# A gated long-convolution backward pass: a key product summed in half-partition VectorE operations, and a PSUM operand in place of an evacuation

## The chip, the cores and the metric

The kernel runs on one core of one Trainium2 chip. The metric is the device time of one execution in microseconds (us). Its engines, as the profile names them: PE is TensorE's matmuls, PEld its weight loads, DVE is VectorE, ACT is ScalarE, POOL is GpSimd, SP issues transfers. Single executions of the kernel before lie within 1.5 us of each other (555.2 to 556.7 us). Each trace is of one execution. The granted clock is the share of full speed that the chip allows TensorE; in before's runs its mean is 0.998 to 1.000.

## The reference, cut to what matters

A forward pass and the gradients of nine of its inputs, in bf16. The forward pass normalises `x`, runs a long convolution over the sequence (2048 positions, 512 channels) by FFT, and gates the result with a sigmoid MLP (512 to 1376 to 512):

```python
kv_f = rfft(k_shift * v, padded)                 # V spectrum
kf_f = rfft(ssm_k, padded)                       # K spectrum (filter)
y    = irfft(kv_f * kf_f)[:S] + kv * ssm_D       # complex product per frequency
s    = q * y                                     # q is the normalised x
g    = silu((sigmoid(xn @ w_gate) * (xn @ w_up)) @ w_down)
out  = x + s * g                                 # then the vector-Jacobian product for grad_out
```

The kernel does the FFTs as matmuls with cosine and sine blocks. Real and imaginary parts lie in the two halves of the 128 partitions, so a complex product is two elementwise products, whose parts have to be added up across the halves. Either the inverse step's matmuls do that (two matmuls per block, one per product), or VectorE does it with half-partition operations, and one matmul per block is enough.

## The kernel before: what the change and the argument touch

Instructions are not emitted as written. A recording layer collects all operations with their dependencies, and a list scheduler lays them out, engine by engine, at build time; the chip then runs that fixed order. Some evacuations may be dealt to ScalarE or VectorE (`evac`), and the parts of the kernel are streams that advance at set paces against each other.

```python
HALF = (1,)                       # which of KK's two halves is summed on VectorE in the backward stage
def evac(self, dst, src, n):      # the scheduler chooses the engine
    self.add([("scalar", "copy", (dst, src), {}), ("vector", "tensor_copy", (dst, src), {})])

def step3(Qf, qq, which, dst):    # second FFT step: 2 matmuls of 512 columns, one evacuation of 1024
    ps = ps_mm([2, 512]); ...     # ps_mm: one of three double PSUM banks in this stage
    nc.evac(dst, ps[:]..., 1024)

def inv3(terms, qq, Bg):          # first inverse step: 8 blocks, one matmul of 128 columns per term
    for g in range(8):
        for n, (Y, r) in enumerate(terms): nc.tensor.matmul(ps[:, g], Y[:, g*128:(g+1)*128], R[:, r], ...)
    nc.evac(...)

def strX():                       # FFT stage: four groups (cg) of four quarter steps (qq)
    for cg in range(NG):
        for qq in range(4): ... step3(QfK, qq, X_RI, KFg[:, qq])        # K spectrum
        for qq in range(5):
            step3(QfV, qq, X_RI, Xc); Y  = Xc * KFg[:, qq]
            step3(QfV, qq, X_IR, Xs); Xs = Xs * KFg[:, qq]              # second product, from SBUF
            inv3(((Y, R_A), (Xs, R_B)), qq - 1, Bg)                     # of the quarter before
        inv1(...)
run_streams([(gG, len(FA) * 11776, 0.05, 0.7), (strK(), 4 * 10240, 0.0, 0.7), (strV(), 4 * 16384, 0.0, 0.8),
             (strX(), 4 * 24576 + 4096, 0.2, 1.0)])     # gG: ten tiles of the gate's matmuls, the filler

def backC():                      # backward stage, beside a stream of weight-gradient matmuls (filler)
    for cg in range(NG):
        for qq in range(5): ...   # two step3 (Xr, Xi), then for KK's halves t = 0, 1:
            # t not in HALF: T2 = K*Xi; K = K*Xr, full height, inv3 with two terms
            # t in HALF: four half-partition products and a sum, inv3 with one term
```

## Time and profile before

556.4 us. The table is worked out from the trace: the price of the matmuls that start in a stretch at 56, 149 and 216 ns for 128, 352 and 512 columns, and the bubbles, the rest of the time from one matmul's start to the next. Time is counted from the first busy instruction, 0.2 us after the trace's span begins; the first matmul starts 2.0 us later, and these 2.0 us stand in no row.

| stretch, us | stage | matmuls at their price | bubbles |
|---|---|---|---|
| 0 to 21 | start-up | 8.4 | 10.7 |
| 21 to 142 | FFT stage, gate tiles beside it | 107.5 | 13.5 |
| 142 to 190 | its end, start of the gated stage | 43.5 | 4.7 |
| 190 to 345 | gated stage | 154.0 | 0.8 |
| 345 to 516 | backward stage | 170.0 | 1.0 |
| 516 to 554 | weight gradients alone | 32.9 | 5.2 |

How to read it: a bubble is the time by which the next matmul starts later than the price says, so the time before the first matmul, the prices and the bubbles make up the whole time. The page's chain that ended last says the same in shares of the span:

```profile
PE 77%; ACT 8%; issue 7%; DVE 5%; POOL 1%; DMA 1%; POOLq 0%; ACTq 0%
```

TensorE carries three quarters of it, and ScalarE's 8% lie almost all before 190 us.

### The profile page before, as it was taken

The numbers are of one execution on the slowest core, as the hardware profiler recorded it, in microseconds if no ns is written. First come the engines' busy times: TensorE is split into PE (matmuls) and PEld (weight loads), VectorE is DVE, ScalarE is ACT, GpSimd is POOL, SyncE is SP. The second block draws the span as 40 slices with busy tenths as digits, with TensorE's granted clock in tenths as the row PEclk, the third lists the DMA queues.
The fourth block names the chain that finished last, engine by engine and source line by source line (L and its number), as shares of the span: only waits on it lengthen the run. The fifth ranks groups of instructions, "written<-read, shape, count | busy, mean of one in ns | idle before, by whom it ended". The sixth has DMA issues, their size and how long they took to land.

```text
span 554.4 us, 13669 instructions
## 1 busy us (share of the span) xinstructions
PE 531.3 (96%) x5613; PEld 377.8 (68%) x5613; DVE 445.1 (80%) x867; ACT 354.1 (64%) x465; POOL 140.6 (25%) x250
## 2 busy tenths in 40 slices
PE   3999899999989999999999999999999999999996
PEld 2999697898778566777665675656756756666544
DVE  9588999856897999889898899739769879798620
ACT  7989999978996234455343445359767858765311
POOL 3234323303212322222232111311041052131221
PEclk9999999999999999999999999999999999999999
DMA  8879889729434898989979979998695588878431
GB/s 288 238 210 279 269 230 295 197 72 282 155 115 111 221 198 211 276 170 201 272 192 274 257 194 301 277 289 238 188 287 174 180 273 254 244 223 247 153 114 37
DMA packets 125288, 120.37 MB, mean 217 GB/s; under 512 B 74963, under 2 KB 104489, under 8 KB 125226
## 3 DMA queue, kind: packets, MB, share of 16 engines
q1 hardware_dynamic: 109946, 71.22, 50.9%
q0 software_dynamic: 14752, 48.27, 27.4%
q8 instruction: 44, 0.72, 0.6%
q14 instruction: 18, 0.15, 0.1%
q10 hardware_dynamic: 528, 0.00, 0.0%
HBM read 54.23 MB, written 47.55 MB: 184 GB/s over the span
## 4 chain that ended last, share of the span: by engine, by line
PE 77%; ACT 8%; issue 7%; DVE 5%; POOL 1%; DMA 1%; POOLq 0%; ACTq 0%
PE psum L515 77%; ACT slab L515 8%; DVE slab L515 5%; POOL out_dram L515 1%; DMA slab<-in_grad_out_dram 1%; POOL slab L515 0%; ACT L515 0%; POOLq L1447 0%; POOLq L515 0%; ACTq L515 0%; POOLq L1436 0%
## 5 line engine op out<-in xcount | busy, mean ns | idle before, releaser
L515 PE MATMUL psum<-slab 128*128 128x128 bf16 (+4 forms) x5613 | 531.3, 257 | 18.6 <-ACT slab L515 11.8
L515 PEld LDWEIGHTS <-slab 128*128 128x128 bf16 (+2 forms) x5613 | 377.8, 102 | 171.8 <-issue 17.6
L515 DVE TENSOR_TENSOR slab<-slab 128x512 bf16<-128x512 bf16 (+5 forms) x507 | 293.6, 623 | 13.9 <-ACT slab L515 6.4
L515 ACT CAST slab<-psum 128x1024 bf16<-128x1024 f32 (+4 forms) x262 | 217.6, 875 | 78.0 <-PE psum L515 68.7
L515 ACT COPY slab<-psum 128x1024 bf16<-128x1024 bf16 (+2 forms) x90 | 75.6, 862 | 90.6 <-PE psum L515 90.4
L515 POOL DMA_DIRECT2D out_dram<-slab x75 | 44.1, 591 | 190.5 <-DVE slab L515 101.9
L515 DVE TENSOR_TENSOR slab<-psum,slab 128x512 bf16<-128x512 f32 (+2 forms) x68 | 44.5, 655 | 26.1 <-PE psum L515 16.3
L515 ACT ACTIVATE slab<-slab 128x512 bf16<-128x512 bf16 (+3 forms) x46 | 36.6, 803 | 15.6 <-DVE slab L515 15.1
L515 ACT ACTIVATE slab<-psum 128x512 bf16<-128x512 f32 (+1 forms) x64 | 37.6, 593 | 11.1 <-PE psum L515 7.7
L515 DVE CAST slab<-psum 128x1024 bf16<-128x1024 f32 (+1 forms) x27 | 31.7, 1181 | 10.2 <-PE psum L515 10.0
L515 DVE SCALAR_TENSOR_TENSOR slab<-slab 128x1 f32<-128x1 f32 (+3 forms) x64 | 28.0, 437 | 12.9 <-ACT slab L515 12.1
L515 POOL DMA_DIRECT2D KK_d<-slab x32 | 17.4, 544 | 58.1 <-ACT slab L515 52.0
L515 POOL DMA_DIRECT2D slab<-in_A_q_dram x29 | 16.0, 553 | 47.2 <-DMA out_dram<-slab 33.2
L515 DVE COPY slab<-psum 128x1024 bf16<-128x1024 bf16 (+1 forms) x26 | 17.1, 667 | 12.8 <-PE psum L515 12.5
L515 DVE TENSOR_SCALAR slab<-slab 128x1 f32<-128x1 f32 (+7 forms) x72 | 20.5, 320 | 0.6 <-ACT slab L515 0.3
L515 DVE SCALAR_TENSOR_TENSOR slab<-psum,slab 128x512 f32<-128x512 f32 x16 | 11.0, 685 | 7.7 <-PE psum L515 7.7
L515 POOL TENSOR_TENSOR slab<-slab 128x1 f32<-128x1 f32 x16 | 11.0, 688 | 14.5 <-DVE slab L515 14.3
L515 POOL DMA_DIRECT2D slab<-in_grad_out_dram x16 | 8.9, 555 | 18.8 <-DMA out_dram<-slab 12.2
L515 POOL DMA_DIRECT2D slab<-slab x8 | 4.5, 565 | 26.5 <-issue 26.5
L515 DVE BATCH_NORM_STATS2 slab<-slab 128x6 f32<-128x512 bf16 x16 | 10.9, 682 | 0.0
L515 POOL DMA_DIRECT2D slab<-in_A_k_dram x12 | 10.2, 848 | 1.3 <-PE psum L515 0.8
L515 POOL MEMSET slab<- 1x384 bf16 (+4 forms) x14 | 5.7, 417 | 8.8 <-DVE slab L515 7.4
(21 smaller groups left out, 38.9 us busy)
## 6 DMA issues: line engine op xcount, KB each, us to landing
KK_d<-slab POOLq DMA_DIRECT2D x32, 256.0 KB, 4.2
slab<-KK_d SPq DMA_DIRECT2D x16, 512.0 KB, 5.2
out_dram<-slab POOLq DMA_DIRECT2D x58, 128.0 KB, 4.2
hS_d<-slab SPq DMA_DIRECT2D x16, 352.0 KB, 3.1
dgS_d<-slab SPq DMA_DIRECT2D x16, 352.0 KB, 3.7
duS_d<-slab SPq DMA_DIRECT2D x16, 352.0 KB, 4.2
slab<-hS_d SPq DMA_DIRECT2D x8, 512.0 KB, 4.8
slab<-dgS_d SPq DMA_DIRECT2D x8, 512.0 KB, 6.4
```

The lines of the kernel that those rows point to most:

```text
L515: getattr(getattr(self.nc, eng), meth)(*[place(v) for v in a], **{x: place(v) for x, v in k.items()})
```

## The change

Its intent: fewer matmuls in the backward stage at the cost of VectorE time, and less evacuation in the FFT stage. Three parts:

```diff
-HALF = (1,)
+def halves(cg, qq):
+    return (0, 1) if qq < 3 else (1,)            # 12 of 16 quarter steps sum both halves of KK on VectorE
 ...  # in f_gen: the transpose of the next tile stands before the first block, not before the third
+            if pi == 0 and n + 1 < NJ and "xnT" not in T[SEQ[n + 1]]:
+                f_xnT(SEQ[n + 1])
-            if pi == 1 and n + 1 < NJ:
-                f_xnT(SEQ[n + 1])
 ...
-    def step3(Qf, qq, which, dst):
+    def step3(Qf, qq, which, dst, by=None):
-        nc.evac(dst, ps[:]..., 1024)
+        if by is None: nc.evac(dst, ps[:]..., 1024)
+        else:          nc.vector.tensor_tensor(dst, ps[:]..., by, ALU.mult)
 ...  # FFT stage
-                    yield from step3(QfV, qq, X_IR, Xs)
-                    nc.vector.tensor_tensor(Xs, Xs, KFg[:, qq], ALU.mult)
+                    yield from step3(QfV, qq, X_IR, Xs, KFg[:, qq])
 ...  # backward stage; n = 2 where both halves are summed, else 1
+                    bc = lambda x: x[:, None, :].to_broadcast([64, n, 1024])
+                    nc.vector.tensor_tensor(T2s[lo, hs], K2[lo, hs], bc(Xr[lo]), ALU.mult)
+                    nc.vector.tensor_tensor(T2s[hi, hs], K2[lo, hs], bc(Xi[lo]), ALU.mult)
+                    nc.vector.tensor_tensor(K2[lo, hs], K2[hi, hs], bc(Xr[hi]), ALU.mult)
+                    nc.vector.tensor_tensor(K2[hi, hs], K2[hi, hs], bc(Xi[hi]), ALU.mult)
+                    nc.vector.tensor_tensor(T2s[:, hs], T2s[:, hs], K2[:, hs], ALU.add)
 ...  # (cuts: the old per-half loop, and inv3's choice of one or two terms)
```

More of the change, by code (lines that the diff above doesn't have):

```diff
@@ L743, in f_gen @@
                 f_ln(SEQ[n + 2])
-            if pi == 1 and n + 1 < NJ:
-                f_xnT(SEQ[n + 1])
-            yield nb * 1024 + (512 if pi == 1 else 0)
+            yield nb * 1024 + (512 if pi == 0 else 0)
         if n < NSP:
@@ L886, in step3 @@
                              start=True, stop=True)
-        nc.evac(dst, ps[:].rearrange("p h x -> p (h x)"), 1024)
+        if by is None:
+            nc.evac(dst, ps[:].rearrange("p h x -> p (h x)"), 1024)
+        else:
+            nc.vector.tensor_tensor(dst, ps[:].rearrange("p h x -> p (h x)"), by, ALU.mult)
         yield 1024
@@ L1268, in backC @@
                     lo, hi = slice(0, 64), slice(64, P)
-                    for t in range(2):
-                        K, T2 = KK[:, t], ys[qq][1][:, t]
-                        if t in HALF:
-                            nc.vector.tensor_tensor(T2[lo], K[lo], Xr[lo], ALU.mult)
-                            nc.vector.tensor_tensor(T2[hi], K[lo], Xi[lo], ALU.mult)
-                            nc.vector.tensor_tensor(K[lo], K[hi], Xr[hi], ALU.mult)
-                            nc.vector.tensor_tensor(K[hi], K[hi], Xi[hi], ALU.mult)
-                            nc.vector.tensor_tensor(T2, T2, K, ALU.add)
-                        else:
-                            nc.vector.tensor_tensor(T2, K, Xi, ALU.mult)
-                            nc.vector.tensor_tensor(K, K, Xr, ALU.mult)
+                    K2, T2s = KK, ys[qq][1]
+                    hv = halves(cg, qq)
+                    if 0 not in hv:
+                        nc.vector.tensor_tensor(T2s[:, 0], K2[:, 0], Xi, ALU.mult)
+                        nc.vector.tensor_tensor(K2[:, 0], K2[:, 0], Xr, ALU.mult)
+                    hs = slice(min(hv), 2)
+                    n = 2 - min(hv)
+                    bc = lambda x: x[:, None, :].to_broadcast([64, n, 1024])
[4 more added lines that the diff above has]
+                    nc.vector.tensor_tensor(T2s[:, hs], T2s[:, hs], K2[:, hs], ALU.add)
                 if qq == 2:
@@ L1284, in backC @@
                     for t, B in ((0, B1), (1, B2)):
-                        yield from inv3(((T2[:, t], R_W),) if t in HALF else ((T1[:, t], R_C), (T2[:, t], R_B)), qq - 1, B)
+                        yield from inv3(((T2[:, t], R_W),) if t in halves(cg, qq - 1) else ((T1[:, t], R_C), (T2[:, t], R_B)), qq - 1, B)
                     ld_KK(cg * 4 + qq + 3)
```

## The prediction

> **What bounds the kernel now.** I read, in this order: the page's first two parts (which engine is full, and when), the waits, the table of stretches, and the groups by shape. Busy time, busy shares and the 40 slices (13.9 us each):
>
> ```profile
> PE 531.3 (96%) x5613; PEld 377.8 (68%) x5613; DVE 445.1 (80%) x867; ACT 354.1 (64%) x465; POOL 140.6 (25%) x250
> ...
> PE   3999899999989999999999999999999999999996
> ...
> DVE  9588999856897999889898899739769879798620
> ACT  7989999978996234455343445359767858765311
> ```
>
> TensorE is nearly always occupied, but a busy matmul row says little, so I checked it against the matmul starts in the trace. From one start to the next, the median is 56 ns for a matmul that streams 128 columns, 149 ns for 352 and 216 ns for 512. With these as the price of one, all 5613 matmuls cost 516.3 us of the 554.4 us span. So about 38 us are bubbles: 2 us before the first matmul, 36 us after it. The table of stretches tells what else is full where those bubbles are. Its columns are busy us (instructions) of PE, PEld, DVE, ACT and POOL, then clock, DMA share and GB/s:
>
> ```profile
> 0.00:21.00 21.00, 12.42 (x134) 10.76 (x135) 17.38 (x65) 16.66 (x18) 5.17 (x18) 1.00 0.95 288
> 21.00:142.00 121.00, 114.31 (x1718) 102.10 (x1716) 99.31 (x158) 112.12 (x142) 38.19 (x68) 1.00 0.77 223
> 142.00:190.00 48.00, 45.14 (x547) 34.49 (x546) 41.17 (x78) 34.27 (x46) 10.83 (x21) 1.00 0.54 154
> 190.00:345.00 155.00, 154.51 (x1523) 103.26 (x1524) 140.11 (x360) 67.85 (x114) 36.60 (x65) 1.00 0.95 229
> 345.00:516.00 171.00, 171.00 (x1517) 110.06 (x1515) 137.73 (x196) 115.59 (x134) 41.02 (x66) 1.00 0.81 237
> 516.00:554.40 38.40, 33.97 (x184) 17.11 (x181) 9.37 (x14) 7.59 (x14) 8.75 (x14) 0.98 0.33 102
> ```
>
> By the same account of starts the bubbles lie here: start-up to 21 us, 10.7 us; FFT stage 21 to 142, 13.5 us; its end and the change to the gated stage 142 to 190, 4.7 us; gated stage 190 to 345, 0.8 us; backward stage 345 to 516, 1.0 us; weight gradients alone to the end, 5.2 us, of which 4.6 us follow the last matmul. So there are **two regimes**. From 190 us on, TensorE streams without a gap: only fewer matmuls help there. In the FFT stage TensorE shares the limit with ScalarE, which is busy 112 of 121 us, 93%. Who holds TensorE there is in the waits of TensorE in the stretch 21 to 142 us:
>
> ```profile
> PE psum L515 <- ACT slab L515: 5.2, 14, 0.8
> PE psum L515 <- DVE slab L515: 0.2, 1, 0.2
> PE psum L515 <- DMA slab<-in_B_w_down_dram: 0.2, 1, 0.2
> ```
>
> It is ScalarE's PSUM evacuations, 14 times; VectorE hardly ever.
>
> **What the Trainium skill says.** (1) "TensorE: Matmul & The Clock Gate", Back-to-back issue gap: warm, N/2.4 + 2.5 ns, so 56 and 216 ns. The trace agrees to the nanosecond; the 81 ns per N=128 pair which the same section gives for real kernels is not what this kernel shows. (2) "VectorE: DVE Perf Modes", The perf-mode tier table: a bf16 tensor product from SBUF runs at two elements per cycle, with any PSUM operand at one. The trace agrees: 686 ns for 1024 elements from SBUF, 685 ns for 512 with one PSUM operand. (3) The same page, Two Vector instructions with no wait between them: an instruction whose inputs or output start in another partition quadrant than the last one's is held until all before it have finished. The trace agrees: full-height products of 1024 start 0.60 us apart, the half-partition ones that alternate halves start 0.71 to 0.72 us apart. (4) "Perfetto Trace Analysis", Identifying the Most-Contended Engine: matmul busy share is no measure of headroom; hence the account by starts above.
>
> **The change, part by part.** The groups that price it, by shape (busy us, mean ns of one; the VectorE and ScalarE rows of the whole run):
>
> ```profile
> L515 ACT CAST slab<-psum 128x1024 bf16<-128x1024 f32 x175 | 172.6, 1037 | 33.6 <-PE psum L515 29.3 <-DVE slab L515 2.2 <-ACT slab L515 0.8
> ...
> L515 DVE TENSOR_TENSOR slab<-slab 128x2048 bf16<-128x2048 bf16 x68 | 82.3, 1219 | 6.5 <-ACT slab L515 3.2 <-DMA slab<-slab 1.6 <-PE psum L515 0.8
> ...
> L515 DVE TENSOR_TENSOR slab<-slab 64x1024 bf16<-64x1024 bf16 x64 | 43.9, 686 | 1.8
> ...
> L515 DVE TENSOR_TENSOR slab<-psum,slab 128x512 bf16<-128x512 f32 x48 | 32.9, 685 | 12.9 <-PE psum L515 7.3 <-ACT slab L515 5.5
> L515 DVE CAST slab<-psum 128x1024 bf16<-128x1024 f32 x25 | 30.4, 1221 | 9.6 <-PE psum L515 9.3
> ```
>
> *Backward stage.* In 12 of 16 quarter steps the product with KK's first half is added up on VectorE, so its inverse step needs one matmul of 128 columns where it needed two: 8 fewer each. 12 x 8 = 96 matmuls x 56 ns = **5.4 us less on TensorE**. The instruction order of the changed kernel confirms the count (5517 against 5613) and shows where the freed time goes: weight-gradient matmuls move forward, and the part after the last 128-column matmul shrinks from 30.1 to 24.7 us at the prices above. VectorE before: two full products (0.60 us apart), four half-partition ones (0.72) and a sum (0.69), 4.8 us per quarter step. After: four half-height ones and a sum over 2048 elements. A row holds 128 partitions or 64 in the same time (686 against 686 ns), and the 2048-element rows of before already have a broadcast operand, so I take 1.22 us each: 5 x 1.22 = 6.1 us. +1.3 us x 12 = +16 us on VectorE. Four 1024-wide evacuations leave VectorE in this stage in the new order, -4.9 us; so +11 us net: 138 to some 149 us of some 170 us, 81% to 88%. Beside work, not on the path, as long as weight-gradient matmuls fill TensorE meanwhile; 24.7 us of them are still left for the end.
>
> *FFT stage.* 16 evacuations of the second product go away (1.04 us on ScalarE, 1.22 us where VectorE did it), and 16 products of 1024 change from SBUF (0.69) to PSUM: 685 ns for 512 plus 512/0.96 = about 1.22 us, an estimate that the CAST row (1221 ns) supports. VectorE: +0.53 x 16 = +8.5 us. The scheduler deals the evacuations out again: in the new order VectorE has 32 of 1024 elements up to the gated stage against 40, but five smaller ones against two. At a mean of 0.95 us (CASTs and COPYs mixed), -7.6 and +1.5: VectorE nearly as before, +2 us. ScalarE loses 8 of 1024, 8.3 us, and three smaller: about -10 of 112 us, 93% to some 85%. ScalarE thus falls below TensorE's own 107.5 us of matmuls in this stage. Of the 13.5 us of bubbles and the 1.9 us at 154 to 159 us (gaps of 0.9, 0.6 and 0.4 us in the same steps of the last group) I expect a third to go: some are bursts in which four evacuations follow each other on ScalarE at 1.02 us while TensorE has 0.43 us of matmuls for each and VectorE is in a row of 2048-element products (56 to 63 us), and these concern the K filter, which the change doesn't touch. My choice: **4 us less**, from 1 to 7.
>
> *Earlier transpose of the normalised tile.* It now stands before the first block's matmuls in place of before the third's; its evacuation (0.6 us) gets some 5 us of matmuls more to hide behind. One short gap looks like it (0.28 us at 173 us). 0.5 us less.
>
> Sum: -5.4 - 4 - 0.5, and +0.5 for short waits on a fuller VectorE in the backward stage: -9.4 us. 556.4 - 9.4 = 547.0.
>
> **The rivals.** (a) *VectorE becomes the bound of the backward stage.* For it: 86% busy between 405 and 435 us already (25.7 of 30), and the chain evacuation, four products, sum, matmul gets 1.3 us longer. Against: TensorE doesn't wait for VectorE once in that stretch, and filler matmuls are at hand. If it came, part of the 5.4 us would be lost: 549 to 552. (b) *The PSUM buffers stick.* A product tile is now held until VectorE reaches it in its order, perhaps behind a row of 1.22 us products, where the evacuation had a choice of two engines; the FFT stage has three double banks. Then the stage gains nothing, or loses 1 to 2 us: 550 to 553. Against: TensorE's waits there are for ScalarE. (c) *ScalarE was the whole limit of the FFT stage*, and its 10 us come out almost in full: 541 to 543. Against: 17 gaps over 0.3 us make up only 8.8 of the 13.5 us, and several stand at K-filter steps and at the sigmoids. (d) *DMA binds*: share 0.8 to 1.0 from 190 us on, but TensorE shows no wait on it after start-up, and the change moves no transfer.
>
> **Range and chances.** The 5.4 us are a count; the FFT stage carries the doubt, and every instruction after it stands in a new order, worth 1 to 2 us either way. Predicted 547.0 us, 8 in 10 between 543.5 and 550.5. Faster by over 2% needs less than 545.3 us, 1.7 us below my number: 0.27. Slower by over 2%, above 567.5: 0.01. Within 2%: 0.72.
>
> **What the profile after would show.** Matmul count 5517 and a sum of 510.9 us at the same prices. 48 rows of 64x2048 at about 1.22 us: near 2.3 us would mean that the broadcast costs the fast mode, and VectorE would bind. 16 products of 1024 from PSUM at about 1.22 us. ScalarE in the FFT stage down by some 10 us. FFT bubbles about 9.5 us in place of 13.5 us. Backward stage: under 2 us of bubbles, no wait of TensorE on VectorE over 1 us. The prediction is wrong if TensorE's waits on VectorE in either stage exceed 3 us, or if the FFT bubbles don't shrink at all, or shrink by more than 7 us.

## The result, and the profile after

550.4 us (550.10 to 550.62, 4 runs) against 556.36 us (556.15 to 556.52, 4 runs): ratio 0.9893, 95% interval 0.9876 to 0.9910. A ratio is the mean time of one kernel's runs over that of the other's of the same rounds, so not quite the ratio of the medians quoted. It is faster by 1.1%, or 6.0 us where 9.4 were expected. That is inside the range of the prediction, but by only 0.1 us (550.5).

The changed kernel's busy times and slices:

```profile
PE 526.4 (96%) x5517; PEld 373.2 (68%) x5517; DVE 458.2 (84%) x831; ACT 350.6 (64%) x461; POOL 140.9 (26%) x250
...
PE   3999899999989999999999999999999999999996
...
DVE  9599999956876999898989998929969999999650
ACT  7888999977985334444443345438868876966411
```

The 96 matmuls are gone and VectorE is fuller, in the last third above all. The same stretches as before (columns as in the prediction):

```profile
21.00:142.00 121.00, 115.66 (x1740) 103.79 (x1738) 103.92 (x156) 107.09 (x136) 39.67 (x69) 1.00 0.77 226
142.00:190.00 48.00, 44.90 (x536) 34.00 (x534) 38.22 (x74) 32.36 (x44) 10.65 (x20) 1.00 0.51 149
...
345.00:516.00 171.00, 170.58 (x1433) 106.50 (x1431) 148.64 (x165) 119.20 (x138) 42.38 (x68) 1.00 0.77 236
```

VectorE in the backward stage stands at 148.6 us of 171, as worked out. The durations hold too (by shape: busy us, mean ns of one):

```profile
L519 ACT CAST slab<-psum 128x1024 bf16<-128x1024 f32 x164 | 161.9, 1029 | 39.4 <-PE psum L519 36.1 <-DVE slab L519 2.3
...
L519 DVE TENSOR_TENSOR slab<-slab 64x2048 bf16<-64x2048 bf16 x48 | 58.5, 1219 | 1.7 <-PE psum L519 0.3
...
L519 DVE TENSOR_TENSOR slab<-psum,slab 128x1024 bf16<-128x1024 f32 x16 | 19.5, 1218 | 0.5 <-issue 0.2 <-PE psum L519 0.2
```

Who made TensorE wait, 21 to 142 us first, then 345 to 516 us:

```profile
PE psum L519 <- ACT slab L519: 4.1, 12, 0.5
PE psum L519 <- DVE slab L519: 0.4, 2, 0.3
```

```profile
PE psum L519 <- ACT slab L519: 0.4, 1, 0.4
```

So no wait moved to VectorE, and ScalarE still holds TensorE up in the FFT stage, for 4.1 us where it was 5.2. The chain that ended last names VectorE more often than before:

```profile
PE 72%; DVE 14%; issue 8%; ACT 5%; POOL 1%; POOLq 0%; ACTq 0%
```

That 14% is no loss in itself: TensorE has 1.5 us of bubbles from 345 to 516 us, because weight-gradient matmuls fill it.

**Where the time went.** Stretches by the clock shift against each other once a kernel is faster, so I compare at equal work: the bubbles that have piled up by the time TensorE has done so many us of matmuls, priced as above. They are taken from the starts of the weight loads, which are complete in every trace (1% of the matmul rows are missing in e1 to e8). In e2 and e4 the granted clock is about one half for 3.4 us in the midst of the work; matmuls take twice their price there, and the table counts that as bubbles too (1.6 and 1.5 us). Worked out from the traces, in us:

| kernel | 50 | 100 | 130 | 150 | 170 | 400 | 480 | all | matmuls |
|---|---|---|---|---|---|---|---|---|---|
| before | 20.1 | 24.2 | 28.4 | 29.6 | 30.8 | 32.1 | 32.5 | 37.9 | 516.3 |
| after | 20.6 | 23.3 | 26.2 | 29.3 | 30.0 | 31.4 | 32.2 | 37.5 | 510.9 |
| e1 backward part only | 19.8 | 23.9 | 28.1 | 29.3 | 30.5 | 31.9 | 33.1 | 38.4 | 510.9 |
| e2 PSUM product only | 22.7 | 25.4 | 28.8 | 31.1 | 31.7 | 32.9 | 33.7 | 39.0 | 516.3 |
| e3 transpose only | 20.6 | 24.4 | 29.2 | 29.8 | 30.5 | 32.2 | 32.6 | 37.9 | 516.3 |
| e4 all 16 quarter steps | 20.3 | 23.2 | 26.0 | 29.1 | 29.8 | 31.2 | 37.6 | 42.9 | 509.1 |
| e5 half the second product | 20.2 | 24.5 | 28.1 | 29.5 | 30.7 | 32.0 | 32.8 | 38.1 | 510.9 |
| e6 half the K evacuations | 20.5 | 23.1 | 26.6 | 28.6 | 29.8 | 31.2 | 32.0 | 37.3 | 510.9 |
| e7 paced | 17.9 | 23.3 | 26.6 | 26.8 | 27.5 | 28.8 | 29.6 | 34.9 | 510.9 |
| e8 before, paced | 20.5 | 25.6 | 29.4 | 30.8 | 31.5 | 32.8 | 33.2 | 38.5 | 516.3 |
| e9 last group as before | 20.7 | 23.3 | 27.1 | 27.6 | 28.3 | 29.8 | 30.5 | 35.8 | 510.9 |
| e10 K stream at 0.6 | 21.5 | 25.7 | 30.7 | 33.0 | 34.2 | 35.4 | 36.3 | 41.6 | 510.9 |
| e11 paced, 13 of 16 | 18.2 | 23.5 | 26.8 | 27.0 | 27.6 | 28.9 | 30.2 | 35.3 | 510.5 |
| e12 paced, no PSUM product | 18.6 | 24.2 | 28.1 | 29.4 | 30.1 | 31.6 | 32.8 | 38.0 | 510.9 |

Read the first two rows: the matmul sum falls by 5.4 us, as counted. The changed kernel is 2.2 us ahead in bubbles at 130 us of work, 0.3 at 150, 0.8 at 170 when the FFT stage is over, 0.4 at the end. I had given the FFT stage and the transpose 4.5 us; they show 0.8. The 2.2 us at 130 overstate the lead: the kernel before has most of the fourth group's bubbles just before that mark (0.8 us each at 154.5 and 156.9 us by the clock), the changed kernel has its own just after it. At 122 us of work, ahead of both, the lead is 1.2 us (26.6 and 25.4), and by 142 it is gone (28.9 in both).

### The profile page after: what moved, and what is told of

The parts are those of the page before. It is cut to its first block, busy times and chain, and to the rows that moved or that the text cites. A ratio compares the mean times of both kernels' runs of the same rounds, so it can differ in the third digit from the quotient of the medians.

```text
span 548.7 us, 13419 instructions
## 1 busy us (share of the span) xinstructions
PE 526.4 (96%) x5517; PEld 373.2 (68%) x5517; DVE 458.2 (84%) x831; ACT 350.6 (64%) x461; POOL 140.9 (26%) x250
## 4 chain that ended last, share of the span: by engine, by line
PE 72%; DVE 14%; issue 8%; ACT 5%; POOL 1%; POOLq 0%; ACTq 0%
PE psum L519 72%; DVE slab L519 14%; ACT slab L519 5%; POOL out_dram L519 1%; POOL slab L519 0%; POOLq L1455 0%; POOLq L519 0%; ACTq L519 0%; POOLq L1444 0%
## 5 line engine op out<-in xcount | busy, mean ns | idle before, releaser
L519 PE MATMUL psum<-slab 128*128 128x128 bf16 (+4 forms) x5517 | 526.4, 258 | 17.9 <-ACT slab L519 10.9
L519 PEld LDWEIGHTS <-slab 128*128 128x128 bf16 (+2 forms) x5517 | 373.2, 102 | 170.7 <-issue 18.7
L519 DVE TENSOR_TENSOR slab<-slab 128x512 bf16<-128x512 bf16 (+7 forms) x467 | 299.6, 683 | 7.9 <-ACT slab L519 3.0
L519 ACT CAST slab<-psum 128x1024 bf16<-128x1024 f32 (+3 forms) x252 | 207.2, 862 | 74.5 <-PE psum L519 65.9
L519 ACT COPY slab<-psum 128x1024 bf16<-128x1024 bf16 (+2 forms) x94 | 80.4, 877 | 90.1 <-PE psum L519 88.5
L519 DVE TENSOR_TENSOR slab<-psum,slab 128x512 bf16<-128x512 f32 (+3 forms) x84 | 63.8, 760 | 23.2 <-PE psum L519 12.6
L519 ACT ACTIVATE slab<-slab 128x512 bf16<-128x512 bf16 (+3 forms) x48 | 38.6, 807 | 16.9 <-DVE slab L519 16.3
L519 DVE CAST slab<-psum 128x1024 bf16<-128x1024 f32 (+1 forms) x21 | 25.1, 1196 | 5.6 <-PE psum L519 5.3
L519 DVE COPY slab<-psum 128x1024 bf16<-128x1024 bf16 (+2 forms) x22 | 13.5, 622 | 10.9 <-PE psum L519 8.6
L519 POOL TENSOR_TENSOR slab<-slab 128x1 f32<-128x1 f32 x16 | 11.5, 716 | 20.3 <-DVE slab L519 20.1
L519 POOL DMA_DIRECT2D slab<-in_grad_out_dram x16 | 8.9, 559 | 26.2 <-DMA out_dram<-slab 14.7
```

The costliest lines, as they stand in the source:

```text
L519: getattr(getattr(self.nc, eng), meth)(*[place(v) for v in a], **{x: place(v) for x, v in k.items()})
```

## The experiments

Twelve runs, five rounds each. **Theory A**: the backward part pays nearly in full, and the FFT stage's bubbles come from the order in which dependent steps stand, so less evacuation there doesn't turn into time. **Rival B**: VectorE gives back part of the backward gain, and the FFT stage delivered. **Rival C**: the PSUM product costs time, and the transpose made up for it. **Rival D**: the two evacuating engines together bound the FFT stage, and too little was taken from them.

### e1 to e3: each part alone

```diff
 # e1: the changed kernel with the PSUM product and the earlier transpose undone
 # e2: only this line of the change
+                    yield from step3(QfV, qq, X_IR, Xs, KFg[:, qq])
 # e3: only this part of the change
+            if pi == 0 and n + 1 < NJ and "xnT" not in T[SEQ[n + 1]]:
+                f_xnT(SEQ[n + 1])
```

> Only the backward part of the change: 12 of 16 quarter steps sum the first product on VectorE; FFT stage and transposes as before. Theory A (the lost part of the expected gain is in the FFT stage; the backward part pays nearly in full): 96 matmuls x 56 ns = 5.4 us less, up to 1 us given back in short gaps of the backward stage, so 551.0 to 552.0 us; bubbles up to 170 us of matmul work within 0.3 us of before (30.8). Rival B (VectorE, 87% busy there, gives back part of the backward gain, and the FFT stage delivered what was expected): 553 us or more, with over 2 us more bubbles between 345 and 516 us than before (1.0).

> Only the second product of the FFT stage from PSUM; the rest as before. Theory A: the stage's evacuation load falls, but little of it reaches the end: 555 to 556.3 us, bubbles up to 170 us of matmul work 29.8 to 30.8 us; the gap to before is larger at 130 us of matmul work (28.4 before) than at 140 to 170. Rival C (the PSUM product itself holds tiles and costs time, and the earlier transpose made up for it): 557 us or more, TensorE's waits on VectorE in the stretch 21 to 142 us over 2 us.

> Only the earlier transpose; the rest as before. Theory A: a small gain of its own, 555.3 to 556.3 us. Rival C: 554 us or less, nearly all that the FFT stage gained in the changed kernel. If it is the order alone that counts, it may also be slower than before, up to 558 us.

Measured, against 556.24 us of before (555.34 to 556.59, 11 runs): e1 551.26 us (551.15 to 551.80), ratio 0.9914 (0.9901 to 0.9927); e2 557.36 us (556.70 to 557.47), ratio 1.0019 (1.0007 to 1.0031); e3 556.21 us (555.07 to 560.33), ratio 1.0014 (0.9991 to 1.0038).

What follows: the backward part alone is worth 5.0 us. Its row of the table is 0.3 us below before up to 170 us of work and 0.6 us above it at 480: 0.9 us of the 5.4 is given back in the backward stage. Rival B falls. The PSUM product alone is 1.1 us **slower**, which I had not expected. The time is rival C's (557 us or more), the mechanism is not: TensorE waits on VectorE for only 0.4 us from 21 to 142 us in that run. It has lost 2.6 us by 50 us of work, and won 1.7 us of them back by 170. Its trace shows a cause that no theory here named. TensorE waits once for 2.0 us, and the granted clock is about one half from 62.8 to 66.3 us (TensorE's row, then that stretch, whose third number from the end is the clock):

```profile
63.12 2.29 PE L519 MATMUL psum<-slab 128*128 128x128 bf16 x17 [2.02 <-ACT slab L519]
```

```profile
62.80:66.30 3.50, 2.96 (x24) 2.63 (x25) 3.09 (x5) 1.28 (x2) 1.08 (x2) 0.51 1.04 300
```

Matmuls of 128 columns start 106 ns apart there in place of 56, which adds 1.6 us to the bubbles although TensorE is at work. All five runs of e2 have a mean granted clock of 0.994 to 0.996. So the 1.1 us are not the price of the PSUM product as such; without the 1.6 us the bubbles at 170 us of work would be 30.1, against 30.8 before (worked out, not run). The transpose alone gives nothing, within a spread of 5.3 us. The two together gain 0.9 us (e1 against the changed kernel; the runs don't overlap, the intervals of the two ratios do). Parts that cost 1.1 and 0 alone and gain 0.9 together don't add up as loads would. A new order, with the clock that it costs, fits; these three runs alone don't show it.

### e4: all sixteen quarter steps

```diff
-    return (0, 1) if qq < 3 else (1,)
+    return (0, 1)
```

> The whole change, but in all 16 quarter steps (also the last of each group) the first product is summed on VectorE: 32 fewer matmuls, 1.8 us less on TensorE, 5.3 us more on VectorE. Theory A with VectorE near its limit in the backward stage: the 1.8 us are more than lost, 552 to 554 us (against 550.4), bubbles between 345 and 516 us from 1.5 to 4 to 7 us, TensorE waiting on VectorE there. If VectorE has room left: 548.6 us.

Measured: 553.88 us (552.54 to 554.11), ratio to before 0.9953 (0.9940 to 0.9966). As expected for a VectorE near its limit: 1.8 us of matmuls less, 3.5 us slower than the change. Bubbles match the changed kernel's up to 400 us of work (31.2 and 31.4) and then grow to 37.6 at 480. TensorE's waits there, 420 to 516 us:

```profile
PE psum L519 <- DVE slab L519: 2.1, 1, 2.1
PE psum L519 <- ACT slab L519: 2.1, 2, 1.7
```

Now a single wait on VectorE is 2.1 us long. After it the granted clock is 0.50 from 514.9 to 518.3 us, which adds 1.5 us. The waits (4.2 us) and this come to 5.7 us, about the 5.6 us of bubbles that e4 adds beyond the changed kernel's between 400 and 480 us of work. So the room that rival (a) of the prediction doubted was there for 12 quarter steps, and not for 16 in this order. That VectorE is full throughout is not shown: from 420 to 500 us it is busy 72.9 of 80 us here and 77.7 in the changed kernel. The new order is a rival that this run doesn't exclude.

### e5 and e6: less evacuation in the FFT stage

```diff
 # e5: second product over 512 of 1024 columns, the rest zero
-            nc.vector.tensor_tensor(dst, ps[:]..., by, ALU.mult)
+            nc.vector.tensor_tensor(dst[:, 0:512], ps[:]...[:, 0:512], by[:, 0:512], ALU.mult)
 # e6: evacuation of the K spectrum over 512 of 1024 columns, the rest zero
+            nc.evac(dst[:, 0:512], ps[:]...[:, 0:512], 512)
```

> The changed kernel, but the second product of the FFT stage is formed over 512 of its 1024 columns only (the rest is zero: wrong result on purpose): 16 x 0.53 = 8.5 us less VectorE work in the FFT stage, the PSUM tiles come free 0.53 us sooner, TensorE work the same. Theory A (the bubbles of the FFT stage come from the order in which the dependent steps stand, not from how much evacuation the two engines have to do): 549.0 to 551.5 us, bubbles at 170 us of matmul work within 1.2 us of the changed kernel's 30.0. Rival D (the two evacuating engines together are the limit of the stage): half of the freed time comes out, 546 to 547 us, bubbles 26 us or less.

> The changed kernel, but the 16 evacuations of the K filter's spectrum take 512 of 1024 columns (wrong result on purpose): some 16 x 0.43 = 7 us less for ScalarE (or VectorE, where it does one) in the very steps at which four evacuations follow each other. Theory A: 548.5 to 551 us, bubbles at 170 us of matmul work 28.8 to 30.5. Rival D: 546 to 547.5 us, bubbles 27 us or less.

Measured (results wrong, as meant): e5 551.07 us (550.62 to 552.12), ratio to before 0.9913 (0.9901 to 0.9926); e6 551.41 us (550.24 to 555.65, a wide set), ratio 0.9925 (0.9899 to 0.9950). The load did fall. The FFT stretch, e5 and then e6, against the changed kernel's 103.92 us of VectorE and 107.09 us of ScalarE:

```profile
21.00:142.00 121.00, 114.04 (x1721) 103.25 (x1730) 97.07 (x156) 107.86 (x136) 39.12 (x68) 1.00 0.79 225
```

```profile
21.00:142.00 121.00, 113.31 (x1715) 102.87 (x1727) 101.04 (x152) 105.24 (x139) 40.05 (x69) 1.00 0.80 226
```

7 us less VectorE work in the one and 5 us less for both engines in the other gave no time at all (e6 is 0.4 us above what theory A allowed); bubbles at 170 us of work are 30.7 and 29.8 against 30.0. Rival D falls in the form in which I put it, that half of the freed time comes out. One reservation: the scheduler knows the shorter operations and lays out another order, so these runs can't hold the order still while the load falls.

### e7, e8, e10, e11 and e12: another order, the same work

```diff
 # e7: backward part and PSUM product, transpose as before; e8: nothing of the change; e12: backward part only
-    run_streams([(gG, len(FA) * 11776, 0.05, 0.7), (strK(), 4 * 10240, 0.0, 0.7), (strV(), 4 * 16384, 0.0, 0.8),
+    run_streams([(gG, len(FA) * 11776, 0.0, 0.7), (strK(), 4 * 10240, 0.0, 0.72), (strV(), 4 * 16384, 0.0, 0.7),
 # e10: the changed kernel with one number altered
-                 (strK(), 4 * 10240, 0.0, 0.7)
+                 (strK(), 4 * 10240, 0.0, 0.6)
 # e11: e7 and one more quarter step summed on VectorE
+    return (0, 1) if qq < 3 or cg == 0 else (1,)
```

> Backward part and PSUM product, transpose where it was, and the four numbers that pace the streams of the FFT stage against each other set anew (gate stream 0.0 to 0.7, K stream to 0.72, V stream to 0.7): not one instruction more or less, only another order. Theory A: the order alone moves the stage by 2 us or more: 546.5 to 549 us, bubbles at 170 us of matmul work 26 to 28.5. Rival D: the work is the same, so is the time: 550 to 551.5 us.

> The kernel before with the same new pace, nothing of the change. Theory A: its own order moves as well, by up to 2 us either way: 554.5 to 557 us; the difference to the run above tells what the change is worth in that order: 7 to 9 us, of which 5.0 us are the backward part, so 2 to 4 us from the PSUM product. If the PSUM product is worth nothing in any order, the difference is 5.0 us.

> The changed kernel with one number altered: the K stream of the FFT stage paced to 0.6 in place of 0.7, the same instructions in another order. Theory A (order, not work, sets the bubbles of the FFT stage): it can be several us slower, 552 to 556 us, all of it before 170 us of matmul work (bubbles there 32 to 36 in place of 30.0), with the busy sums of ScalarE and VectorE over the run within 5 us of the changed kernel's. Rival D (amount of evacuation): 550 to 551 us.

> The paced version with the first product summed on VectorE in 13 of 16 quarter steps in place of 12 (the last of the first group too): 8 fewer matmuls, 0.45 us, against 1.3 us more VectorE work in the first group of the backward stage. If VectorE has room there: 547.4 to 547.8 us (paced: 548.0). If not: 548 to 549 us.

> The paced version without the PSUM product (backward part alone, new pace, transpose where it was). It sizes the PSUM product in the paced order directly. From before_paced (554.8) less the backward part (5.0): 549.8 us, bubbles at 170 us of matmul work 29 to 31.5 in place of the paced version's 27.5. If the PSUM product is worth nothing in this order either: 548.0 us and bubbles of 27.5 us.

| run | us, median (range) | ratio to before (95%) |
|---|---|---|
| e7 paced | 548.02 (547.51 to 548.26) | 0.9853 (0.9840 to 0.9866) |
| e8 before, paced | 554.84 (554.02 to 556.88) | 0.9983 (0.9966 to 1.0000) |
| e10 K stream at 0.6 | 556.18 (554.58 to 556.71) | 1.0001 (0.9987 to 1.0014) |
| e11 paced, 13 of 16 | 547.86 (547.72 to 548.11) | 0.9855 (0.9840 to 0.9870) |
| e12 paced, no PSUM product | 551.33 (549.65 to 553.87) | 0.9926 (0.9903 to 0.9949) |

The order alone moves the time by more than the whole FFT part was expected to. One pacing number takes the changed kernel from 550.4 to 556.2 us (e10): all that the change gained. Its busy sums stay within 3.1 us of the changed kernel's (ScalarE 353.7 against 350.6, VectorE 456.4 against 458.2), while 4.2 us of bubbles are added before 170 us of work in its profile, which fell on the fastest of its five runs (554.58 us). Three of the others, 1.5 to 1.9 us slower, have a mean granted clock of 0.995 or 0.996, so a stretch of half clock as in e2 may be part of their time; no trace of them was kept. Another pace (e7) takes 2.5 us of bubbles off. The bubbles of both are within the expectations of theory A, and so is e7's time; e10's median is 0.2 us above the 552 to 556 us.

In the new order the PSUM product is worth 551.33 - 548.02 = 3.3 us (e12 against e7), or 2.6 us by the bubbles at 170 us of work (30.1 and 27.5); in the old order it cost 1.1 us, slower clock included. Between e8 and e7 the two parts together are worth 6.8 us, where I had expected 7 to 9. My expectation for e12 was 549.8 us, so the backward part seems worth only 554.84 - 551.33 = 3.5 us in that order; e8 and e12 spread by 3 to 4 us between runs, and e8's profile is of its slowest run, so I rest nothing on this. e11 can't be told from e7 (0.16 us). e7 and e11 are faster than both kernels: 1.5% under before, some 2.4 us under the changed kernel.

### e9: where the FFT stage gave its gain back

In the changed kernel the lead is lost between 122 and 142 us of work, most of it after 130, which is the fourth group, 155 to 169 us by the clock, when the gate tiles are used up. TensorE there, before:

```profile
155.49 1.80 PE L515 MATMUL psum<-slab 128*128 128x512 bf16 x18 [0.75 <-ACT slab L515]
157.75 1.96 PE L515 MATMUL psum<-slab 128*128 128x128 bf16 x20 [0.45 <-ACT slab L515]
159.90 8.27 PE L515 MATMUL psum<-slab 128*128 128x128 bf16 x142 [0.19 <-ACT slab L515]
```

And in the changed kernel, TensorE and then VectorE's rows of the second product (start, us; in brackets the idle time before and what ended it):

```profile
157.32 3.97 PE L519 MATMUL psum<-slab 128*128 128x128 bf16 x52 [0.46 <-DVE slab L519]
162.41 5.27 PE L519 MATMUL psum<-slab 128*128 128x512 bf16 x59 [1.12 <-ACT slab L519]
```

```profile
156.04 1.23 DVE L519 TENSOR_TENSOR slab<-psum,slab 128x1024 bf16<-128x1024 f32 x1 [0.24 <-issue]
...
160.32 1.23 DVE L519 TENSOR_TENSOR slab<-psum,slab 128x1024 bf16<-128x1024 f32 x1
```

TensorE restarts at 157.32 us just after the first of these ends (157.27), and it stands for another 1.1 us around the second, which the profile puts down to ScalarE. So the theory F of this run: without filler the 1.22 us product is a step of the chain.

```diff
-                    yield from step3(QfV, qq, X_IR, Xs, KFg[:, qq])
+                    yield from step3(QfV, qq, X_IR, Xs, KFg[:, qq] if cg < 3 else None)
+                    if not (cg < 3):
+                        nc.vector.tensor_tensor(Xs, Xs, KFg[:, qq], ALU.mult)
```

> The changed kernel with the last of the four groups of the FFT stage in the old form (second product evacuated, then multiplied from SBUF); the first three as changed. The order up to some 100 us of matmul work is the same. Theory F (the changed kernel is 2.3 us ahead of before at 130 us of matmul work and loses that by 140 because the last group's product, 1.22 us on VectorE, stands in the chain of dependent steps when no gate tile is left to fill TensorE): bubbles at 140 to 170 us of matmul work 1 to 2 us fewer than the changed kernel's 28.9 to 30.0, time 548.5 to 549.5 us. If the loss sits there for another reason: bubbles at 170 us of matmul work 29.5 to 30.5, time 550 to 551 us.

Measured: 548.80 us (547.84 to 551.42), ratio to before 0.9880 (0.9861 to 0.9900). Bubbles match the changed kernel's to within 0.1 us up to 120 us of work (25.1 and 25.2), then 27.6 at 150 and 28.3 at 170, against 29.3 and 30.0. TensorE in the same stretch:

```profile
153.38 2.00 PE L519 MATMUL psum<-slab 128*128 128x128 bf16 x20 [0.53 <-ACT slab L519]
155.82 12.36 PE L519 MATMUL psum<-slab 128*128 128x128 bf16 x183 [0.44 <-DVE slab L519]
```

From 155.8 us on it runs through. Theory F holds as expected in the bubbles: with the old form in that group they end 1.7 us lower. The times alone would not prove it (e9's runs spread by 3.6 us, and the intervals of the ratios, 0.9861 to 0.9900 and 0.9876 to 0.9910, overlap). The order of the group changes along with the form, and in e7 the new form stands in the last group too and loses little there (26.6 at 130, 26.8 at 150). So it is this form in this order, not the form as such.

## Why the prediction was right, and where it was off, point by point

- *Two regimes, TensorE the bound from 190 us on.* Right: the matmul sum fell from 516.3 to 510.9 us, and bubbles after 170 us of work went from 7.1 to 7.5 us (37.9 - 30.8 and 37.5 - 30.0).
- *Backward part: -5.4 us, +0.5 given back.* Right in count and size: e1 measures 5.0 us; in the changed kernel bubbles grow by 2.2 us from 170 to 480 us of work, before by 1.7. The 30.1 and 24.7 us after the last 128-column matmul come from the instruction order; in the traces they are 26.4 and 21.0, the same 5.4 us less.
- *VectorE +11 us to 149 us, 64x2048 at 1.22 us.* Right: 148.6 us, 1.219 us. Rival (a) stayed away for 12 quarter steps; at 16 (e4) TensorE waits on VectorE once for 2.1 us.
- *PSUM product 1.22 us; ScalarE some 10 us less, VectorE +2.* Right for the duration (1.218 us), too much for ScalarE. From 21 to 142 us it falls by 5.0 us, to 107.1 of 121 (89% where I had said 85%). From 21 to 170 us ScalarE is busy 7.2 us less and VectorE 1.7 us more, as that stretch of before and then after shows:

```profile
21.00:170.00 149.00, 140.83 (x2067) 123.72 (x2065) 123.09 (x190) 138.12 (x172) 44.91 (x81) 1.00 0.70 204
```

```profile
21.00:170.00 149.00, 141.20 (x2072) 124.59 (x2070) 124.76 (x183) 130.90 (x163) 46.13 (x81) 1.00 0.69 205
```

- *"I expect a third to go ... My choice: 4 us less".* This is the step that failed. Measured: 0.8 us at 170 us of work, the transpose included, so under the range of 1 to 7 us as well. By the prediction's own account of starts the bubbles from 21 to 142 us are 11.9 us; 9.5 were expected, 13.5 stood before. The total came inside the range because the counted part came almost whole. I took ScalarE's 93% as the limit of the stage and let part of its relief come out. The runs put another thing in its place: with this scheduler the stage's bubbles hang on the fixed order. Less evacuation gave nothing (e5, e6), and the same work in another order gave -2.5 to +4.2 us of bubbles (e7, e10). The 1.2 us that the change had gained by 122 us of work were lost in the fourth group, and e9 gets 1.7 us back there.
- *Transpose: -0.5 us.* Not seen: alone 556.21 against 556.24 us.
- *Rival (b), "The PSUM buffers stick".* Its size came true for the part alone (+1.1 us), its mechanism did not show: 0.4 us of waits on VectorE, but one wait of 2.0 us put down to ScalarE and 3.4 us at half clock.
- *"every instruction after it stands in a new order, worth 1 to 2 us either way".* Too small: e10 lost 5.8 us by one pacing number (4.2 us in its fastest run).

What stays open: which property of an order makes it good, and whether less evacuation would pay with the order held still. Only the fourth group's loss and e2's long wait were located.

## What to carry to other kernels

Where one engine streams without a gap and has filler, a change is worth nearly the instructions that it takes from that engine (5.0 of 5.4 us here), and these can be counted. Where several engines take turns through short dependent steps in a fixed order, a busy share of 93% on one of them doesn't say what its relief is worth: measure one part alone, and then the same work in another order, before the gain is put down to the work. After such a change it can pay to set the pacing of the streams anew; here that was worth another 2.4 us. Look at the granted clock in every trace: after single waits of 2.0 and 2.1 us (e2, e4) it was one half for 3.4 us, and cost 1.6 and 1.5 us more; a wait of 1.7 us in e10's trace was not followed by it.

## What the Trainium skill lacked or had wrong

- "TensorE: Matmul & The Clock Gate", Back-to-back issue gap: it gives some 81 ns per matmul of 128 columns and 131 ns for 512 in a real kernel, and calls the formula one for isolated matmuls. Here, in a full kernel with a weight load before each matmul, the median gaps are 56 and 216 ns, the formula's.
- "Perfetto Trace Analysis", Identifying the Most-Contended Engine: occupancy is called a fair measure of the distance to the limit for Vector and Scalar. ScalarE at 112 of 121 us looked like a limit. The change took 5.0 us off it there and e6 another 1.9 us (and 2.9 us off VectorE), and the bubbles at 170 us of work went only from 30.8 to 30.0 and 29.8 us. The order moved as well, so this doesn't refute the sentence; it shows how little the share said here. The section on strategy says to look for the gaps; no page that I read says how much a fixed order of dependent steps can cost (here up to 5.8 us of 550 from one pacing number).
- "VectorE: DVE Perf Modes", The perf-mode tier table: no row for half the partitions with a repeated operand. Here 64x2048 with an operand repeated along the outer free dimension took 1.219 us, like the 128x2048 rows (1.219 us).
